# Unit 1's bonus sum in front of its masks, and unit 0's decayed k behind unit 2's bonus product

## The chip, the cores and the metric

One Trainium2 chip, one core. The metric is the device time of one execution in microseconds (us), median of several runs; lower is better. The kernel had been tuned already. Engines: TensorE (PE in the profile), VectorE (DVE), ScalarE (ACT), GpSimd (POOL), and SyncE (SP), which issues most transfers.

## The reference, cut to what matters

```python
def _attn_ref(r, k, v, w, u):            # B, H, S, D = 4, 8, 768, 48
    state = zeros(B, H, D, D)
    for t in range(S):
        cur = einsum('bhd,bhe->bhde', u * k_t, v_t)            # the "bonus" of the step itself
        y[:, :, t] = einsum('bhd,bhde->bhe', r_t, state + cur)
        state = w * state + einsum('bhd,bhe->bhde', k_t, v_t)
    return y

def _moe_ref(x, w_in, w_out):            # x: 3072 x 384, d_ff = 2048
    h = x @ w_in
    return (h * sigmoid(h)) @ w_out
```

The output is the second function applied to the first one's y. The kernel works on units, a unit being 128 steps of one batch (24 units, 4 for each stretch of 128 steps). For each it transposes r and k and scales them by powers of w, multiplies them to scores, masks the scores, multiplies by v to y, adds the bonus, transposes y and feeds it to the two dense layers. The bonus of a row is v times the sum over d of r·u·k.

## The kernel before

The parts that matter here; what each engine runs is in the order of emission.

```python
    def nat_ku(i):      # GpSimd
        nc.gpsimd.tensor_tensor(out=L["ku"], in0=kin[i % NIN][:, :, 0:D], in1=u_bc, op=ALU.mult)
    def nat_rk(i):      # GpSimd: the bonus product
        nc.gpsimd.tensor_tensor(out=L["rku_f"], in0=rin[i % NIN][:, :, 0:D], in1=L["ku"], op=ALU.mult)
    def nat_kc(i):      # GpSimd: decayed k, read by sums(i) only
        nc.gpsimd.tensor_tensor(out=kc[i % NKC][:, :, 0:D], in0=kin[n][:, :, 0:D], in1=lamC, op=ALU.mult)
    def bonus_sum(i):   # VectorE
        nc.vector.tensor_reduce(out=L["rku"], in_=L["rku_f"], axis=mybir.AxisListType.X, op=ALU.add)
    def bonus_vu(i):    # GpSimd
        nc.gpsimd.tensor_tensor(out=L["vu"], in0=vin[i % NIN], in1=L["rku"]...broadcast, op=ALU.mult)
    # p1(i): TensorE transposes r and k (tr, tk), VectorE scales both into rk
    # p2(i): TensorE scores ae, ao; VectorE masks them into am (two instructions)
    # p3y(i): TensorE y = am times v; p3e(i): VectorE y16 = y + vu
    # p4(i): TensorE transposes y16, ScalarE copies it to xT
    # fill(n): n portions of first- or second-layer matmuls; spin(n): n dummy matmuls
    # [...]
    bonus_act(0)
    nc.scalar.copy(out=st[1], in_=zero)
    win_part(512, 1024)
    p2(1, spins=2)
    bonus_sum(1)
    bonus_vu(1)
    p3e(0)
    nat_kc(0)
    spin(3)
    p3y(1)
    p3e(1)
    spin(2)
    p4(0)
    p1(2)
    nat_ku(2)
    nat_rk(2)
    win_part(1024, 1536)
    win_part(1536, 2048)
    nc.gpsimd.memset(rin[B][:, 0, 0:1], 0.0)   # holds the next loads back
    load(B)
    load(B + 1)
    p4(1)
    # [...]
    spin(2)
    fillers.extend(l1s(0, 0, 2))
    fill(.5)
    nat_v(2)
    bonus_sum(2)
    bonus_vu(2)
    p2(2)
    fill(1.5)
    p3y(2)
    # [...] later
    wout_part(0)
    sums(1)
    state(1)
    bonus_sum(b_)
    bonus_vu(b_)
    nat_kc(b_)
    wout_part(1)
```

Of the kernel before, what the change touches and what calls it, by code (L numbers as in the profile page):

```python
# [15 lines left out]
def kernel(  # L16
# [101 lines left out]
    def spin(n, t=None):  # L118

        if t is None:  # L120
            t = ps.tile([128, 512], FP, name="spin", tag="t", bufs=5)
        else:
            t = t.rearrange("s p t -> s (p t)")
        for _ in range(n):
            nc.tensor.matmul(t, junk[:, 0:128], junk, start=True, stop=True)
# [51 lines left out]
    def nat_ku(i):  # L177
        L = live.setdefault(i, {})
        L["ku"] = wrk.tile([128, H, D], FP, name="ku")
        nc.gpsimd.tensor_tensor(out=L["ku"], in0=kin[i % NIN][:, :, 0:D], in1=u_bc,  # L180
                                op=ALU.mult)

    def nat_rk(i):
        L = live[i]
        L["rku_f"] = wrk.tile([128, H, D], FP, name="rku_f")
        nc.gpsimd.tensor_tensor(out=L["rku_f"], in0=rin[i % NIN][:, :, 0:D], in1=L["ku"],  # L186
                                op=ALU.mult)

    def nat_kc(i):
        n = i % NIN  # L190
        nc.gpsimd.tensor_tensor(out=kc[i % NKC][:, :, 0:D], in0=kin[n][:, :, 0:D],  # L191
                                in1=lamC, op=ALU.mult)

    def bonus_sum(i):
        L = live[i]
        L["rku"] = wrk.tile([128, H], FP, name="rku", bufs=3)
        nc.vector.tensor_reduce(out=L["rku"], in_=L["rku_f"], axis=mybir.AxisListType.X,  # L197
                                op=ALU.add)

    def bonus_vu(i):  # L200
        L = live[i]
        L["vu"] = wrk.tile([128, H, D], FP, name="vu", bufs=3)
        nc.gpsimd.tensor_tensor(out=L["vu"], in0=vin[i % NIN],  # L203
                                in1=L["rku"].unsqueeze(2).broadcast_to([128, H, D]),
                                op=ALU.mult)
# [26 lines left out]
    def p1t(i):  # L232

        n = i % NIN
        L = live.setdefault(i, {})
        xs = [ps.tile([128, 2, NP, 64], FP, name="xs", tag="t", bufs=5) for _ in range(2)]
        for a, src in enumerate((rin, kin)):
            flat = src[n].rearrange("p h d -> p (h d)")
            for p in range(NP):
                for g in range(2):  # L240
                    t = slice(64 * g, 64 * g + 64)
                    nc.tensor.transpose(xs[g][0:PR, a, p, :],  # L242
                                        flat[t, 128 * p:128 * p + PR], ident[t, t])
        rk = wrk.tile([PR, 2, NP, C], FP, name="rk")
        L["rT"] = rk[:, 0]
        L["kT"] = rk[:, 1]
        L["xs"] = xs, rk

    def p1d(i):
        L = live[i]  # L250
        xs, rk = L["xs"]
        for g in range(2):
            nc.vector.tensor_tensor(out=rk[:, :, :, 64 * g:64 * g + 64], in0=xs[g][0:PR],  # L253
                                    in1=lam(g), op=ALU.mult)
# [6 lines left out]
    def p2(i, spins=0, nxt=None, late=False):  # L261
        L = live[i]
        ae = ps.tile([128, NP, C], FP, name="ae", tag="t", bufs=5)
        ao = ps.tile([128, NP, C], FP, name="ao", tag="t", bufs=5)
        spin(spins, ae)
        for p in range(NP):
            nc.tensor.matmul(ae[:, p, :], L["kT"][0:D, p, :], L["rT"][0:D, p, :],  # L267
                             start=True, stop=True)
            nc.tensor.matmul(ao[:, p, :], L["kT"][64:PR, p, :], L["rT"][64:PR, p, :],  # L269
                             start=True, stop=True)  # L270
        if nxt is not None:
            p1t(nxt)
        L["am"] = []
        for a in (ae, ao):
            am = wrk.tile([128, NP, C], F16, name="am", bufs=4)
            nc.vector.tensor_tensor(out=am, in0=a,  # L276
                                    in1=maskM.unsqueeze(1).broadcast_to([128, NP, C]),
                                    op=ALU.mult)
            L["am"].append(am)
        if nxt is not None and not late:  # L280
            p1d(nxt)

    def p3y(i):
        sc, b = unit(i)
        L = live[i]
        v16 = L["v16"]
        L["y"] = y = ps.tile([128, H, D], FP, name="y", tag="t", bufs=5)
        for p in range(NP):
            if sc:
                nc.tensor.matmul(y[:, 2 * p:2 * p + 2, :], L["rT16"][:, p, :],  # L290
                                 st16[b][:, p, :], start=True, stop=False)
            for j in range(2):
                nc.tensor.matmul(y[:, 2 * p + j, :], L["am"][j][:, p, :],  # L293
                                 v16[:, 2 * p + j, :], start=not sc,
                                 stop=(not sc or j == 1))

    def p3e(i):
        L = live[i]
        L["y16"] = wrk.tile([128, H, D], F16, name="y16")
        nc.vector.tensor_tensor(out=L["y16"], in0=L["y"], in1=L["vu"], op=ALU.add)  # L300
# [33 lines left out]
    def p4(i):  # L334
        sc, b = unit(i)
        L = live[i]
        if sc not in xts:
            xts[sc] = wrk.tile([128, NQ, B, C], F16, name="xT", bufs=3)
        yT = ps.tile([128, NQ, C], F16, name="yT", tag="t", bufs=5)
        yf = L["y16"].rearrange("p h d -> p (h d)")  # L340
        for q in range(NQ):
            nc.tensor.transpose(yT[:, q, :], yf[:, 128 * q:128 * q + 128], ident16)  # L342
        nc.scalar.copy(out=xts[sc][:, :, b, :], in_=yT)  # L343
# [68 lines left out]
    def win_part(c0, c1):  # L412
        nc.gpsimd.dma_start(out=win[:, :, c0:c1],
                            in_=moe_w_in[:, c0:c1].rearrange("(q p) n -> p q n", p=128))
# [27 lines left out]
    bonus_act(0)  # L442
    nc.scalar.copy(out=st[1], in_=zero)
    win_part(512, 1024)
    p2(1, spins=2)
    bonus_sum(1)
    bonus_vu(1)
    p3e(0)
    nat_kc(0)
    spin(3)  # L450
    p3y(1)
    p3e(1)
    spin(2)
    p4(0)
    p1(2)
    nat_ku(2)
    nat_rk(2)
    win_part(1024, 1536)
    win_part(1536, 2048)
    nc.gpsimd.memset(rin[B][:, 0, 0:1], 0.0)  # L460
# [174 lines left out]
```

## Time and profile before

| | before |
|---|---|
| median of the first 3 runs | 202.49 us (202.49 to 202.76) |
| TensorE busy | 193.5 of 201.0 us |
| unit 2's seven y matmuls start | 20.62 us |
| TensorE idle just before them | 0.40 us |

TensorE is nearly full, so the time is its work plus the few places where it waits. Of its 7.5 us without work, 4.5 lie in the first 66 us and the rest behind its last matmul. The prediction shows the lines.

### The profile page before, as it was taken

Reading aid. Unit: us, or ns where it says so; the run is one execution under the profiler, and the core shown is the slowest. Engines: PE = TensorE matmul, PEld = TensorE weight load, DVE = VectorE, ACT = ScalarE, POOL = GpSimd, SP = SyncE. Lnnn points to the kernel's source line nnn. Section 1 sums busy time; section 2 is a strip of 40 time slices with the busy share of each in tenths; the row PEclk is TensorE's granted clock in tenths of the full one; section 3 lists DMA queues with packets and bytes.
Section 4 is the critical chain, followed back from the end, with each engine's and each line's share of the span. In section 5 each row is a group of like instructions: output and inputs, shape, how many; then the busy total and the mean of one; then the engine's idle time right before and its main releaser. Section 6 shows DMA issues by size and latency. Waiting matters only on the chain.

```text
span 201.0 us, 5015 instructions
## 1 busy us (share of the span) xinstructions
PE 193.5 (96%) x1973; PEld 130.5 (65%) x1973; DVE 115.2 (57%) x233; ACT 98.0 (49%) x225; POOL 115.0 (57%) x145
## 2 busy tenths in 40 slices
PE   7989999999999999999999999999999999999993
PEld 2756778777766876675666765666764666744563
DVE  6686658885659439594646864646863635510121
ACT  2375587789232660139662038662029661069300
POOL 3479969979965764867683757481748370100000
PEclk9999999999999999999999999999999999999999
DMA  4999999999989961678731739201120001210022
GB/s 86 198 183 163 156 235 177 170 188 202 175 171 213 250 122 49 150 157 186 144 67 42 156 99 179 43 0 42 39 83 0 0 3 41 74 46 0 0 78 78
DMA packets 82207, 22.34 MB, mean 111 GB/s; under 512 B 75400, under 2 KB 82184, under 8 KB 82184
## 3 DMA queue, kind: packets, MB, share of 16 engines
q1 hardware_dynamic: 78504, 18.88, 43.9%
q0 software_dynamic: 3680, 3.15, 10.2%
q8 instruction: 15, 0.25, 0.5%
q14 instruction: 8, 0.07, 0.1%
HBM read 20.45 MB, written 4.72 MB: 125 GB/s over the span
## 4 chain that ended last, share of the span: by engine, by line
PE 84%; POOL 7%; issue 4%; DVE 2%; ACT 1%; POOLq 0%; DVEq 0%
PE ops L366 30%; PE hps L354 28%; PE ae L267 11%; PE xs L242 4%; PE y L293 2%; PE yT L342 2%; PE y L290 2%; POOL rku_f L186 2%; POOL ku L180 1%; PE sps L309 1%; PE ops L380 1%; DVE am L276 1%; POOL kc L191 1%; DVE y L300 1%; POOL vu L203 1%
## 5 line engine op out<-in xcount | busy, mean ns | idle before, releaser
L357 ACT ACTIVATE gT<-hps 128x256 f16<-128x256 f32 (+1 forms) x128 | 59.5, 493 | 24.6 <-PE hps L354 22.8
L354 PE MATMUL hps<-xT,win 128*128 128x256 f16 (+1 forms) x384 | 69.9, 326 | 0.9 <-ACT xT L343 0.4
L366 PE MATMUL ops<-wout,gT 128*128 128x384 f16 x368 | 65.5, 326 | 0.0
L354 PEld LDWEIGHTS <-win 128*128 128x128 f16 x384 | 35.1, 98 | 22.7 <-issue 1.7
L366 PEld LDWEIGHTS <-gT 128*128 128x128 f16 x368 | 34.3, 98 | 21.1
L343 ACT COPY xT<-yT 128x384 f16<-128x384 f16 x24 | 11.4, 476 | 58.2 <-PE yT L342 58.2
L276 DVE TENSOR_TENSOR am<-ae,maskM 128x512 f16<-128x512 f32 x24 | 16.6, 691 | 35.9 <-PE ao L269 35.8
L203 POOL TENSOR_TENSOR vu<-vin,rku 128x384 f32<-128x384 f32 x23 | 19.0, 828 | 19.9 <-DVE rku L197 19.8
L370 DVE COPY osb<-ops 128x384 f32<-128x384 f32 x23 | 12.8, 555 | 29.2 <-PE ops L366 29.0
L267 PE MATMUL ae<-rk 48*128 48x128 f32 x192 | 27.7, 285 | 0.0
L269 PE MATMUL ao<-rk 48*128 48x128 f32 x192 | 27.7, 285 | 0.0
L267 PEld LDWEIGHTS ae<-rk 48*128 48x128 f32 x192 | 23.1, 187 | 7.1 <-issue 5.5
L253 DVE TENSOR_TENSOR rk<-xs,pif 112x512 f32<-112x512 f32 x40 | 25.6, 680 | 1.7 <-PE xs L242 1.7
L186 POOL TENSOR_TENSOR rku_f<-rin,ku 128x384 f32<-128x384 f32 x24 | 24.1, 1005 | 1.9
L180 POOL TENSOR_TENSOR ku<-kin,u_bc 128x384 f32<-128x384 f32 x24 | 24.1, 1002 | 1.8 <-DMA kin<-in_k_dram 1.5
L191 POOL TENSOR_TENSOR kc<-kin,lamC 128x384 f16<-128x384 f32 x24 | 24.0, 1000 | 0.0
L269 PEld LDWEIGHTS ao<-rk 48*128 48x128 f32 x192 | 23.1, 187 | 0.0
L323 POOL CAST stb<-st 112x384 f16<-112x384 f32 x12 | 6.0, 502 | 25.9 <-DVE st L318 25.9
L300 DVE TENSOR_TENSOR y<-y,vu 128x384 f16<-128x384 f32 x24 | 13.3, 554 | 9.2 <-PE y L293 6.7
L276 DVE TENSOR_TENSOR am<-ao,maskM 128x512 f16<-128x512 f32 x24 | 16.3, 680 | 0.0
L197 DVE TENSOR_REDUCE rku<-rku_f 128x8 f32<-128x384 f32 x24 | 13.2, 550 | 2.8 <-POOL rku_f L186 2.4
L325 POOL TENSOR_TENSOR sdec<-st,pif 112x384 f32<-112x384 f32 x16 | 13.3, 835 | 2.2 <-ACT gT L357 1.1
(74 smaller groups left out, 190.5 us busy)
## 6 DMA issues: line engine op xcount, KB each, us to landing
rin<-in_r_dram SPq DMA_DIRECT2D x24, 192.0 KB, 3.7
kin<-in_k_dram SPq DMA_DIRECT2D x24, 192.0 KB, 3.9
vin<-in_v_dram SPq DMA_DIRECT2D x24, 192.0 KB, 3.7
out_dram<-osb SPq DMA_DIRECT2D x23, 192.0 KB, 2.0
win<-in_moe_w_in_dram POOLq DMA_DIRECT2D x4, 384.0 KB, 5.8
wout<-in_moe_w_out_dram POOLq DMA_DIRECT2D x2, 768.0 KB, 10.3
out_dram<-osh SPq DMA_DIRECT2D x1, 128.0 KB, 1.7
out_dram<-osh SPq DMA_DIRECT2D x1, 64.0 KB, 1.5
```

The lines of the kernel that those rows point to most:

```text
L180: nc.gpsimd.tensor_tensor(out=L["ku"], in0=kin[i % NIN][:, :, 0:D], in1=u_bc, op=ALU.mult)
L186: nc.gpsimd.tensor_tensor(out=L["rku_f"], in0=rin[i % NIN][:, :, 0:D], in1=L["ku"], op=ALU.mult)
L191: nc.gpsimd.tensor_tensor(out=kc[i % NKC][:, :, 0:D], in0=kin[n][:, :, 0:D], in1=lamC, op=ALU.mult)
L203: nc.gpsimd.tensor_tensor(out=L["vu"], in0=vin[i % NIN], in1=L["rku"].unsqueeze(2).broadcast_to([128, H, D]), op=ALU.mult)
L253: nc.vector.tensor_tensor(out=rk[:, :, :, 64 * g:64 * g + 64], in0=xs[g][0:PR], in1=lam(g), op=ALU.mult)
L267: nc.tensor.matmul(ae[:, p, :], L["kT"][0:D, p, :], L["rT"][0:D, p, :], start=True, stop=True)
L269: nc.tensor.matmul(ao[:, p, :], L["kT"][64:PR, p, :], L["rT"][64:PR, p, :], start=True, stop=True)
L276: nc.vector.tensor_tensor(out=am, in0=a, in1=maskM.unsqueeze(1).broadcast_to([128, NP, C]), op=ALU.mult)
L300: nc.vector.tensor_tensor(out=L["y16"], in0=L["y"], in1=L["vu"], op=ALU.add)
L354: nc.tensor.matmul(hps, win[:, q, ft * 128:(ft + 1) * 128], xts[sc][:, q, b0:b1, :].rearrange("p b t -> p (b t)"), start=(q == 0), stop=(q ...
L357: nc.scalar.activation(out=gts[sc][:, ft, b0 * C:b1 * C], in_=hps, func=AF.Silu)
L366: nc.tensor.matmul(ops, gts[sc][:, ft, b * C:(b + 1) * C], wout[:, ft, :], start=(ft == 0), stop=(ft == NFT - 1))
```

## The change

Its intent: GpSimd waits 1.2 us for unit 1's bonus sum, which stands behind two masks on VectorE; the sum is put in front of them. Unit 0's decayed k, which nobody needs soon, stands in front of unit 2's bonus product; it is put behind. One dummy matmul moves from behind unit 1's y to before it.

```diff
     bonus_act(0)
     nc.scalar.copy(out=st[1], in_=zero)
     win_part(512, 1024)
-    p2(1, spins=2)
     bonus_sum(1)
     bonus_vu(1)
+    p2(1, spins=2)
     p3e(0)
-    nat_kc(0)
-    spin(3)
+    spin(4)
     p3y(1)
     p3e(1)
-    spin(2)
+    spin(1)
     p4(0)
     p1(2)
     nat_ku(2)
     nat_rk(2)
+    nat_kc(0)
     win_part(1024, 1536)
```

## The prediction

> **What bounds the kernel now.** I read the page first, then the busy time by stages, the chain that ended last, and for 10 to 30 us the order of instructions on each engine. From the page:
>
> ```profile
> PE 193.5 (96%) x1973; PEld 130.5 (65%) x1973; DVE 115.2 (57%) x233; ACT 98.0 (49%) x225; POOL 115.0 (57%) x145
> PEclk9999999999999999999999999999999999999999
> ```
>
> TensorE is busy for 193.5 of 201.0 us at full clock. The busy time by stages tells where the missing 7.5 us lie:
>
> ```profile
> 0.00:20.00 20.00, 17.62 (x135) 10.99 (x135) 13.93 (x41) 10.10 (x28) 12.73 (x27) 1.00 0.88 158
> 20.00:60.00 40.00, 38.32 (x490) 30.57 (x490) 27.18 (x54) 26.43 (x73) 35.14 (x41) 1.00 1.06 184
> 100.00:150.00 50.00, 50.00 (x532) 32.74 (x531) 31.64 (x62) 20.25 (x41) 29.12 (x35) 1.00 0.32 76
> ```
>
> The first two times are the stretch and TensorE's busy part of it. TensorE lacks 2.4 us in the first 20, 1.7 us in the next 40 and nothing in the middle. The change touches only orders between 12 and 20 us, so the question is by how much TensorE's dense work after that starts earlier, and whether later waits swallow it. The chain that ended last, in order of time, says what the start hangs on:
>
> ```profile
> 12.99 0.74 POOL win L413
> 13.73 1.17 issue
> ...
> 14.95 0.82 POOL vu L203
> 15.77 0.97 POOL kc L191
> 16.73 0.96 POOL ku L180
> ...
> 17.78 1.01 POOL rku_f L186
> ...
> 18.81 0.04 DVE rku L197
> ...
> 19.28 1.29 DVE am L276 x2
> 20.57 0.05 issue
> 20.62 0.35 PE y L293 x7
> ```
>
> Until 20.6 us it runs through GpSimd, then over unit 2's bonus sum and two masks on VectorE to unit 2's y, and from there almost wholly through TensorE. VectorE's order of instructions has the two places that matter:
>
> ```profile
> 13.11 0.69 DVE L276 TENSOR_TENSOR am<-ae,maskM 128x512 f16<-128x512 f32 x1 [0.79 <-PE ao L269]
> 13.72 0.68 DVE L276 TENSOR_TENSOR am<-ao,maskM 128x512 f16<-128x512 f32 x1
> 14.31 0.54 DVE L197 TENSOR_REDUCE rku<-rku_f 128x8 f32<-128x384 f32 x1
> ...
> 18.81 0.55 DVE L197 TENSOR_REDUCE rku<-rku_f 128x8 f32<-128x384 f32 x1 [1.26 <-POOL rku_f L186]
> 19.28 0.68 DVE L276 TENSOR_TENSOR am<-ae,maskM 128x512 f16<-128x512 f32 x1
> ```
>
> Unit 1's sum waits behind unit 1's masks although its input was ready at 12.99 (the product ran 11.99 to 12.99); GpSimd waits 1.2 us for it. Unit 2's sum waits for GpSimd until 18.81, and unit 2's masks wait behind it although TensorE's last score matmul started at 18.63 and took 0.27, so that they could start at about 18.93. TensorE then idles for 0.40 us before unit 2's y at 20.62.
>
> **What the Trainium skill says.** "GPSIMD Engine Reference", section 3.1, gives about 2.6 cycles an element for two inputs: at its 1.2 GHz, 384 elements take 832 ns. The trace has 828 for vu, but 1,000 to 1,005 for ku, the k-r product and kc, whose inputs are padded rows; I use the trace's. "VectorE: DVE Perf Modes", section "The perf-mode tier table", gives tensor_reduce only its slowest mode; the trace has 0.54 us for the sum, and the next instruction starts 0.46 us after it, which is what moving it costs or frees. "TensorE: Matmul & The Clock Gate", Part 1, lets the clock fall after an idle window of some 3.4 us; the gaps here are 0.2 to 0.8 us and the granted clock is full in every slice, so I give a few tenths of idle no further price. "DMA: Bandwidth & Descriptors", section "Queues, rings and completion order", says that the DMA engines take turns between queues packet by packet; see the third rival.
>
> **The change part by part.** Nothing is added or removed: the dummy matmuls stay five (3 and 2 become 4 and 1), and the number of buffers taken and their order are the same.
>
> Part 1, unit 1's sum ahead of its masks. The sum starts at 13.02, just after its input (unit 2's started within 0.02 us of its own: 18.81 after 17.78 + 1.01). VectorE is idle from 12.3 to 13.11, so of its 0.46 us pitch 0.09 falls into idle time and the masks move from 13.11 to 13.49: 0.38 later. Masks at 13.49 and 14.09 to 14.78 (pitch 0.60), unit 1's y on TensorE at 14.84 instead of 14.46, done at 15.19. Unit 0's addition follows the masks at 14.69 instead of 14.77, so its transpose starts 0.08 earlier, at 15.30. On GpSimd the vu of unit 1 is free of its wait once the win issue is out (12.93 to 13.73): it runs 13.77 to 14.6 instead of 14.95 to 15.77. Unit 1's addition now waits for y and not for vu: 15.24 instead of 15.80, 0.56 earlier. The transposes of unit 2 go 0.08 earlier (15.47, 15.91), and VectorE's scalings of them run at 16.12 and 16.72 instead of 16.28 and 16.87. So 0.38 us is spent in front of y and what follows is still 0.08 to 0.16 earlier.
>
> Part 2, kc of unit 0 behind unit 2's product. kc takes 0.97 us of GpSimd; its only reader is unit 0's sums at 29.99, so it has over 10 us of slack. Unit 2's ku would start at 14.56, but its k has to land first. The view of DMA issues around 7.4 us has it:
>
> ```profile
> kin<-in_k_dram SPq DMA_DIRECT2D x1, 192.0 KB, 7.5
> ```
>
> Issued at 7.39, landed at about 14.9. So ku runs 14.95 to 15.95 (before: 16.73), the product 16.03 to 17.03 (before: 17.78 to 18.79), then kc to 18.0, the two win issues to 19.55, and the memset that opens the loads of units 4 and 5 at 19.6 instead of 20.29.
>
> Together, at unit 2: its sum no longer waits and follows the scalings at 17.3 to 17.86, in time in which VectorE was idle. The first layer's matmuls before unit 2's scores depend on unit 1's output copy, 0.08 earlier, so the last score is done at about 18.85. The masks start there instead of at 19.28: 0.43 earlier. They end at 20.13, and y comes at 20.19 instead of 20.62. vu of unit 2, 19.6 to 20.4, is ready before y ends at 20.54.
>
> TensorE's path from y on: before the change it idled for 0.22 at 26.07 (ScalarE's cast of v), 0.22 and 0.40 at 39.62 and 40.53, 0.27 at 48.41, 0.39 at 65.58, and not at all from there to 197. I followed each back: the cast runs behind gT, which waits for TensorE's own hps; the next two are y to addition to transpose and transpose to copy; the one at 48.41 goes through GpSimd's sdec and vu, which began at VectorE's state copies after unit 5's y; the last is ScalarE behind the transpose of unit 9. All hang on TensorE's earlier work, so they move with it and swallow nothing. The sum: 20.62 - 20.19 = 0.43 us, 202.49 - 0.43 = 202.06. I say 202.05.
>
> The parts aren't additive. Either alone takes most of unit 2's wait away. Part 1 alone leaves the product ready at about 17.6, still ahead of the scores; part 2 alone has it at about 17.83, and costs no delay of unit 1's masks.
>
> **Rivals.**
> 1. The wait only moves to unit 1: the masks' 0.38 us delay goes straight through to unit 2, and the result is 202.5 to 202.9. For it: y of unit 1 was on VectorE's masks already. Against it: before, 0.54 us of sum stood between masks and unit 0's addition, and unit 1's addition waited for vu until 15.80; both fall away.
> 2. A new wait at y of unit 2. If k lands a microsecond later than I read, ku starts at 15.9, the product ends at 18.0, still ahead of 18.85. If the masks wait instead on the first-layer matmuls before the scores, most stays. 202.1 to 202.3.
> 3. The DMA. The win parts and loads of units 4 and 5 start 0.7 us earlier. In before, DMA had a hole at 19 to 20.5 us (share 0.11 and 0.48) because these issues came late; it may be filled, or the win parts may take turns with unit 3's last loads. GpSimd waited 1.47 us for k of unit 4, until 27.40, but TensorE's transposes of it came only at 28.08. An earlier landing frees GpSimd and not TensorE: 202.0 to 202.1.
> 4. The whole 1.75 us by which the k-r product of unit 2 comes earlier reaches the end: 200.7. Against it, the scores' end at 18.85 is a floor that no order of GpSimd moves.
>
> **Range and chances.** The three runs of before lie 0.27 us apart, so a gain of 0.43 is little more than that. 201.7 holds a gain a little better than mine through the DMA; 202.6 holds rival 1 in part. Two per cent is 4 us, and TensorE lacks only 7.5 us in the whole span, most of it not touched. Faster or slower by that is 1 in 100 each.
>
> **What would show each step.** Right: unit 1's sum at 13.0 and masks at 13.5; vu of unit 1 at 13.8; ku of unit 2 at about 14.9 with a wait for k; unit 2's masks released by TensorE's scores and not by the sum, near 18.85; its y near 20.2; about 0.4 us less TensorE idle in the first 20.6 us and the same waits later. Wrong: unit 2's y still at 20.6; a new idle time of TensorE before 60 us, as on a load or on kc in unit 0's sums; or a span that differs by more than the shift of y.

## The result, and the profile after

| | before | changed |
|---|---|---|
| median | 202.62 us (202.49 to 202.83, 4 runs) | 202.14 us (202.14 to 202.26, 3 runs) |
| ratio, 95% | | 0.9977 (0.9958 to 0.9997) |
| profiled span | 201.0 us | 200.4 us |
| unit 2's y | 20.62 us | 20.02 us |

A ratio is the mean time of one kernel's runs over that of the other's of the same rounds, so not quite the ratio of the medians. One more run of the changed kernel took 223.65 us at a granted clock of 0.854 and is left out here; with it the median of the four is 202.2. The gain is 0.2%, and near the predicted 0.43 us (the medians differ by 0.48).

VectorE's order after, from the view of instructions in order of time (start, duration, what, and in brackets the idle time before it with what ended it):

```profile
12.85 0.55 DVE L197 TENSOR_REDUCE rku<-rku_f 128x8 f32<-128x384 f32 x1 [0.77 <-POOL rku_f L186]
13.32 0.68 DVE L276 TENSOR_TENSOR am<-ae,maskM 128x512 f16<-128x512 f32 x1
...
17.14 0.54 DVE L197 TENSOR_REDUCE rku<-rku_f 128x8 f32<-128x384 f32 x1
18.68 0.69 DVE L276 TENSOR_TENSOR am<-ae,maskM 128x512 f16<-128x512 f32 x1 [1.00 <-PE ao L269]
```

Unit 1's sum is now in front of the masks. Unit 2's sum (17.14) waits for nobody, and unit 2's masks are released by TensorE's scores and no longer stand behind the sum: VectorE was idle for 1.00 us before them. GpSimd, same view:

```profile
12.76 0.80 POOL L413 DMA_DIRECT2D win<-in_moe_w_in_dram  x1
13.58 0.84 POOL L203 TENSOR_TENSOR vu<-vin,rku 128x384 f32<-128x384 f32 x1
14.38 1.00 POOL L180 TENSOR_TENSOR ku<-kin,u_bc 128x384 f32<-128x384 f32 x1
15.46 1.01 POOL L186 TENSOR_TENSOR rku_f<-rin,ku 128x384 f32<-128x384 f32 x1
16.43 1.00 POOL L191 TENSOR_TENSOR kc<-kin,lamC 128x384 f16<-128x384 f32 x1
```

No bracket is left: the wait of 1.21 us before vu is gone, kc stands behind the product, and the product ends at 16.47 (before: 18.78). And TensorE at the two y:

```profile
14.06 0.20 PE L293 MATMUL y<-v,am 128*128 128x48 f16 x1 [0.25 <-DVE am L276]
14.66 0.35 PE L293 MATMUL y<-v,am 128*128 128x48 f16 x7 [0.40 <-DVE am L276]
...
20.02 0.35 PE L293 MATMUL y<-v,am 128*128 128x48 f16 x7 [0.27 <-DVE am L276]
```

Unit 1's y pays a new 0.25 us of idle time; unit 2's idles for 0.27 instead of 0.40.

**A part of the 0.60 us between the profiles is luck of the start.** Everything in the changed profile is 0.24 us early already at unit 0's first mask (9.14 against 9.38 us), long before the first changed instruction. The same four transposes of unit 0's r show why, before and then after:

```profile
5.37 1.06 PE L223 MATMUL tr<-ident,rin 128*112 128x128 f32 x4
```

```profile
5.10 0.60 PE L223 MATMUL tr<-ident,rin 128*112 128x128 f32 x4
```

Four equal instructions take 1.06 us in one run and 0.60 in the other. The Trainium skill, "TensorE: Matmul & The Clock Gate", Part 1, describes this: TensorE starts at half its clock until a free-running activity window has passed, so the moment differs from run to run. The traces show it: their record of the full clock begins 7.09 us after the start of the span before the change and 4.81 us after it. (The views print 1.00 for the time ahead of that record as well.) In 14 profiles the record begins between 4.35 and 7.59 us. Where it begins by 6.65 us, the first mask starts at 9.13 to 9.15 us; where it begins at 6.87 us or later, the mask starts at 9.26 to 9.44. So from here on my measure for this stage is **the time from unit 0's first mask to unit 2's seven y matmuls**: 20.62 - 9.38 = 11.24 us before, 20.02 - 9.14 = 10.88 after. The change is worth 0.36 us there; the other 0.24 of the profiles' 0.60 is the start. Behind that point nothing is lost or won: the waits of TensorE at 26.07, 39.62, 40.53, 48.41 and 65.58 us come back at 25.48, 39.03, 39.94, 47.82 and 65.00 with the same lengths to 0.01 us, and from unit 2's y to the end of the span it is 180.38 us in both.

One sign of the prediction did not show, "about 0.4 us less TensorE idle". Between the first mask and unit 2's seven y, TensorE's idle time by the record fell from 1.29 to 1.20 us only. Of the 0.36 us, 0.21 lie ahead of the first y matmul, and the record counts them as busy time: the first y started 1.18 us after the nine first-layer matmuls in front of it had begun (18.84 to 20.02), and starts 0.99 us after that now (18.58 to 19.57). The other 0.15 lie between the first y and the seven.

### The profile page after: what moved, and what is told of

Same layout as the page of the kernel before. It is cut to its first block, busy times and chain, and to the rows that moved or that the text cites. A ratio compares the mean times of both kernels' runs of the same rounds, so it can differ in the third digit from the quotient of the medians.

```text
span 200.4 us, 5014 instructions
## 1 busy us (share of the span) xinstructions
PE 192.2 (96%) x1973; PEld 129.8 (65%) x1973; DVE 115.1 (57%) x233; ACT 98.1 (49%) x225; POOL 115.1 (57%) x145
## 3 DMA queue, kind: packets, MB, share of 16 engines
q1 hardware_dynamic: 78504, 18.88, 43.7%
## 4 chain that ended last, share of the span: by engine, by line
PE 86%; issue 4%; POOL 4%; DVE 3%; ACT 2%; POOLq 0%; DVEq 0%
PE ops L366 30%; PE hps L354 29%; PE ae L267 11%; PE xs L242 4%; PE y L293 3%; PE yT L342 2%; PE y L290 2%; PE sps L309 1%; PE ops L380 1%; DVE am L276 1%; POOL rku_f L186 1%; POOL ku L180 1%; DVE y L300 1%; ACT xT L343 1%; PE ao L269 1%
```

## The experiments

Twelve kernels ran, all correct but the last, which is wrong on purpose (the record has no e9). A scatter of 0.3 to 2.5 us within one kernel remains in the timings (runs of the kernel before reach from 202.46 to 204.39 in these jobs), so the measure in the profile decides, and the times are given beside it. Each ratio is to the runs of before of the same job.

| kernel | measure (us) | median (us) | ratio to before, 95% |
|---|---|---|---|
| before | 11.24 | 202.67 (11 runs, first job) | |
| changed, run again (e12) | 10.83 | 202.23 | 0.9971 (0.9948 to 0.9993) |
| e1 sum (with the dummy) alone | 10.82 | 202.39 | 0.9976 (0.9952 to 1.0000) |
| e2 kc alone | 10.91 | 202.54 | 0.9989 (0.9969 to 1.0009) |
| e3 before, unit 2's sum behind its masks | 10.91 | 202.82 | 1.0011 (0.9987 to 1.0036) |
| e4 before, kc twice | 12.32 | 203.64 | 1.0035 (0.9997 to 1.0072) |
| e5 changed, two kc in front | 11.60 | 202.92 | 0.9998 (0.9967 to 1.0029) |
| e6 changed, three kc in front | 12.61 | 203.88 | 1.0047 (1.0009 to 1.0085) |
| e7 changed, dummies as before | 10.87 | 202.73 | 0.9999 (0.9977 to 1.0022) |
| e8 transposes of unit 2 first | 10.26 | 201.96 | 0.9958 (0.9922 to 0.9993) |
| e10 changed, weights issued early | 10.93 | 202.33 | 0.9969 (0.9945 to 0.9993) |
| e11 e8 with weights issued early | 10.26 | 202.00 | 0.9980 (0.9942 to 1.0019) |
| e13 e11 with loads left out | 10.21 | 201.61 | 0.9944 (0.9924 to 0.9964) |

In e8, e11 and e13 the seven matmuls follow the first of unit 2's y without a gap. Their start is taken as 0.20 us ahead of the next transposes, as it is after the change (20.02 and 20.22).

### e1: the first part alone

```diff
-    nat_kc(0)            # behind nat_rk(2), as in the changed kernel
+    nat_kc(0)            # in front of nat_ku(2), as in before
```

> Part 1 alone: unit 1's sum in front of its masks, unit 0's kc still in front of unit 2's product. My measure is the time from unit 0's first mask to unit 2's seven y matmuls: 11.24 us in before, 10.88 in the changed kernel. Theory (the scores' end is the floor, both parts overlap): the product ends about 1 us before the scores do, unit 2's masks are released by the scores, the measure is 10.88 within 0.1, and the time is 0.3 to 0.5 us under before. Rival (the move of kc is what pays): 11.2 and no gain.

The dummy matmul stays moved here as in the changed kernel, so this is the sum and the dummy together. Measured: 10.82, as in the changed kernel. Unit 2's sum waits 0.23 us for the product, until 17.65, and the masks start at 18.88, released by the scores. Sum and dummy take the whole stage gain; the rival falls. The median is 0.28 us under before.

### e2: the second part alone

```diff
 (kernel before)
     p3e(0)
-    nat_kc(0)
 ...
     nat_rk(2)
+    nat_kc(0)
```

> Part 2 alone: kc behind unit 2's product, unit 1's sum behind its masks as in before. Theory: vu of unit 1 stays late (its wait for the sum about 1.2 us stays), the product of unit 2 ends about 1.0 us earlier than in before, in front of the scores; the measure is 10.9 within 0.1 and the time 0.25 to 0.5 us under before. Rival (unit 1's sum is what pays): the measure stays at 11.2.

Measured: 10.91, so either part alone frees unit 2's masks. The median is only 0.13 us under before, not the 0.25 to 0.5 expected. In the profile a little is given back. vu of unit 2 stays late, unit 2's addition waits 1.01 us for it (until 20.99), and unit 3's y comes 16.46 us after the first mask, against 16.34 in the changed kernel and 16.28 in e1. The profile also met a wait that none before it had shown:

```profile
50.20 0.81 PE L366 MATMUL ops<-wout,gT 128*128 128x384 f16 x4 [0.28 <-DMA wout<-in_moe_w_out_dram]
```

TensorE waits for the second part of the second layer's weights. By the reckoning under e7 the ninth of these matmuls started 0.45 us late, and the profiled span is 201.0 us as before. This was not in my prediction; e7 and e10 to e13 go after it.

### e3: the wait itself taken away in another place

```diff
 (kernel before)
-    bonus_sum(2)
-    bonus_vu(2)
     p2(2)
+    bonus_sum(2)
+    bonus_vu(2)
```

> Before with one edit: unit 2's sum and vu behind its masks, nothing else moved. Theory: unit 2's masks were held by the sum alone, so they start with the scores, 0.35 us earlier, and y of unit 2 too (measure 10.9); but vu of unit 2 now waits for the late sum and ends near 21.5 us, so unit 2's addition, unit 3's scalings and scores come late and the gain is given back there: 0.0 to 0.2 us against before. Rival (the masks waited for the scores or something else): the measure stays at 11.2.

Measured: 10.91, and unit 3's y 16.86 after the first mask, 0.17 later than in before (16.69). The view of VectorE:

```profile
18.70 0.69 DVE L276 TENSOR_TENSOR am<-ae,maskM 128x512 f16<-128x512 f32 x1 [1.38 <-PE ao L269]
...
19.91 0.54 DVE L197 TENSOR_REDUCE rku<-rku_f 128x8 f32<-128x384 f32 x1
21.39 0.56 DVE L300 TENSOR_TENSOR y<-y,vu 128x384 f16<-128x384 f32 x1 [0.94 <-POOL vu L203]
```

With the sum out of their way the masks start with the scores: so in the kernel before it was the late sum, and through it GpSimd, that held them. The gain is then given back at unit 2's addition, as expected. Freeing the masks alone is worth nothing; vu has to come early too.

### e4, e5, e6: a known amount of GpSimd time in front of unit 2's product

```diff
 (e4: kernel before)          (e5, e6: changed kernel, kc in front of nat_ku(2), none behind)
     nat_kc(0)                +    nat_kc(0)      # e5: twice, e6: three times
+    nat_kc(0)                     nat_ku(2)
```

> Before with unit 0's kc computed twice (same result), in front of unit 2's product. Theory: GpSimd's chain into unit 2's sum was critical and what is lost there reaches the end one to one: measure 12.2 and time 203.5 to 203.7, about 0.97 us over before. Rival (later slack takes it up): under 0.4 us.

> The changed kernel with two kc of unit 0 in front of unit 2's product and none behind it. Theory: the product had about 2.2 us of slack to the scores' end less the sum's 0.46, so two kc (1.96 us) overshoot by 0.23 us: measure 11.1, time 0.1 to 0.3 us over the changed kernel. Rival (the slack is less, kc costs at once): 1 us or more.

> The changed kernel with three kc in front of unit 2's product. Theory: now GpSimd sets unit 2's masks again, 1.2 us later than in the changed kernel: measure 12.1, time 203.3 to 203.6. Rival (something else than sum or scores holds the masks): less than 0.6 us.

e4: two kc took 2.07 us instead of 0.99, 1.08 more, and the measure grew by 1.08. The profiles keep it to the end: unit 3's y comes 1.08 later too, and from the first mask to the end of the span it is 192.8 us for 191.6. So the chain through GpSimd was critical, one to one. By times this is weaker: the medians differ by 0.97, but the interval of the ratio just includes no change, as runs of before scatter up to 204.39.

e5 and e6 came out 0.5 above what I expected (11.60 and 12.61 for 11.1 and 12.1). Two causes show in the profiles. First, GpSimd itself started later in these two runs: its first work waits for unit 1's r to land, 8.00 and 7.90 us against 7.59 in the changed kernel's profile. Part 1 of the change has VectorE's masks of unit 1 wait behind a sum that waits for GpSimd, so this passes on (unit 1's sum at 13.25 in e5, 12.85 in the changed profile). Second, kc after kc took 1.08, not 0.98. The size was off, the mechanism was not:

```profile
18.93 0.55 DVE L197 TENSOR_REDUCE rku<-rku_f 128x8 f32<-128x384 f32 x1 [1.31 <-POOL rku_f L186]
19.40 0.68 DVE L276 TENSOR_TENSOR am<-ae,maskM 128x512 f16<-128x512 f32 x1
```

This is e5: the sum waits for GpSimd again and the masks follow it without a wait of their own, as in the kernel before. By dose, with 0, 1, 2 and 3 kc in front of the product the measure is 10.88, 10.82, 11.60 and 12.61: no cost for the first, 0.8 to 1.0 for each further one, the late starts included. The floor is TensorE's scores.

### e7: the dummy matmuls

```diff
-    spin(4)
+    spin(3)
     p3y(1)
     p3e(1)
-    spin(1)
+    spin(2)
```

> The changed kernel with the dummy matmuls as in before (3 and 2 and not 4 and 1). Theory: they lie in idle time of TensorE and do nothing: measure 10.88 within 0.1, time that of the changed kernel within 0.15 us. Rival (the fourth one keeps TensorE from something or warms it): a shift of one dummy matmul, 0.2 us.

The measure is 10.87, and yet the dummy matters. In this profile GpSimd was early by chance: unit 1's sum starts 3.55 us after the first mask and not 3.71 as in the changed kernel, its masks gain as much, but unit 2's scalings gain only 0.02 (6.78 for 6.80). TensorE shows where the rest was lost, first the changed kernel (its seven y start at 14.66), then e7:

```profile
14.85 0.38 PE L125 MATMUL spin<-junk 128*128 128x512 f16 x1
15.12 0.34 PE L342 MATMUL yT<-ident,y 128*128 128x128 f16 x3
```

```profile
14.48 0.35 PE L293 MATMUL y<-v,am 128*128 128x48 f16 x7 [0.40 <-DVE am L276]
14.67 0.59 PE L125 MATMUL spin<-junk 128*128 128x512 f16 x2
15.10 0.33 PE L342 MATMUL yT<-ident,y 128*128 128x128 f16 x3
```

Unit 0's output transposes (yT) start 0.46 us after unit 1's seven y with one dummy between them, 0.62 with two. From unit 1's sum to unit 2's y it is 7.17 us in the changed kernel, e1, e10 and e12, and 7.32 in e7. So behind the delayed y a second dummy costs 0.15 us, and moving it is a part of the gain. My expectation was wrong and the rival (0.2 us) about right; with the sum at 3.71, e7 would be at some 11.03 (an estimate, 3.71 + 7.32).

The median is 202.73, 0.34 over e1 in the same job. The profiled run, one of 202.44, also has the same wait as e2's:

```profile
48.29 1.46 PE L366 MATMUL ops<-wout,gT 128*128 128x384 f16 x8
49.92 0.81 PE L366 MATMUL ops<-wout,gT 128*128 128x384 f16 x4 [0.17 <-DMA wout<-in_moe_w_out_dram]
```

The ninth second-layer matmul needs the second half of the weights. Undisturbed, twelve of these take 2.11 us and the last 0.326, so one follows another after (2.11 - 0.326) / 11 = 0.162 us and the ninth starts 1.30 after the first: at 49.59 here. The weights landed at 49.84 (issued 38.04, 11.8 us). The same sum for the others: before, needed 50.21, landed 49.85; changed, needed 49.63, landed 49.57; e2, needed 49.75, landed 50.11. In these profiles the kernel before was 0.36 us clear of this wait and the changed one 0.06; e12, the changed kernel again, was 0.64 clear (needed 49.68, landed 49.04), so the clearance scatters from run to run. I had not looked for it, because a wait of zero length stands in no list.

Whether the dummy's 0.15 us and this wait make up all of e7's slower times is not shown: only one of its six runs was profiled.

### e12: the changed kernel again; e10: the weights issued earlier

```diff
 (e10)
     wout_part(0)
+    wout_part(1)
     sums(1)
     state(1)
     bonus_sum(b_)
     bonus_vu(b_)
     nat_kc(b_)
-    wout_part(1)
```

> The changed kernel again, unchanged, for more rounds beside e10 and e11 on one chip. Theory: the time to unit 2's y is the same in every run (measure 10.88 within 0.1), and what scatters is the start of TensorE and a wait for the second part of the second layer's weights near 49.7 us, which its profile missed by 0.05 us and e7, whose order is the same but for the dummies, hit by 0.2. So 202.1 to 202.9, median 202.3 to 202.5, and a profile that shows 0 to 0.3 us of idle there. Rival (the dummy split of e7 costs something): no run over 202.4.

> The changed kernel with the second part of the second layer's weights issued right behind the first, 2.5 us earlier on GpSimd. Theory (their landing is the next thing that TensorE runs into): landed at least 1 us before TensorE needs them, no wait there, measure 10.88 unchanged, median 0.05 to 0.3 us under that of e12. Rival (the wait is a chance of single runs, or the DMA engines are full and it lands no earlier): no difference from e12, or unit 5's vu comes late and costs 0.2.

e12 repeats the result: measure 10.83, median 202.23, five of six runs at 202.13 to 202.28 and one at 202.84. Its weights landed at 49.04, and TensorE had no wait there. The rival, a cost of e7's dummies, is right by e7's trace (0.15 us), and the medians point the same way (202.23 against 202.73, from different jobs); only its "no run over 202.4" failed.

e10 refutes my theory, as far as one profile can. The second part was issued 2.5 us earlier (35.6 for 38.14) and landed later, not earlier (50.1 for 49.04 in e12 and 49.57 in the changed kernel's first profile):

```profile
L417 POOL DMA_DIRECT2D wout<-in_moe_w_out_dram x2: 881/909/937, 34.6 to 35.6; - x2
...
DMA to landing us min/median/max: 10.1/12.3/14.5
```

This is e10's view of the weights' tile: the two issues start at 34.6 and 35.6, and the longest landing is the second's. 35.6 + 14.5 = 50.1 us, with 0.31 us of wait on TensorE. Nothing is gained by the issue: it only waits longer.

### e8: an attempt at a better version; e11: the same with the weights early

```diff
 (e8, on top of the change)
     p3e(1)
-    spin(1)
+    p1(2)
     p4(0)
-    p1(2)
 ...
-    fill(.5)
     nat_v(2)
     bonus_sum(2)
     bonus_vu(2)
     p2(2)
-    fill(1.5)
+    fill(2)
```

> An attempt at a better version on top of the change: unit 2's transposes on TensorE ahead of unit 0's output transposes, and the first layer's three matmuls before unit 2's scores put behind them. Theory (what bounds now is transposes, scalings, scores of unit 2): scalings about 0.45 us earlier, scores released by the scalings at about 16.9 us, measure 10.25 within 0.15, time about 0.6 us under the changed kernel, near 201.6. Rival (unit 0's and 1's output copies or the loads of unit 2 hold TensorE instead): no gain, or a loss of some tenths.

> The version of e8 (transposes of unit 2 first) with the weights issued early as in e10. Theory: measure 10.27 as in e8, no wait for the weights, 0.5 to 0.7 us under e12, near 201.7. Rival (the two gains don't add since the weights' issue delays unit 5): no better than e8's 201.96.

e8's measure is 10.26, 0.62 below the changed kernel, and unit 3's y comes 15.72 us after the first mask instead of 16.34. In the changed kernel the scores began at 17.49, behind three first-layer matmuls that had waited for unit 1's output copy (until 17.02); unit 2's scalings ended at 17.22. e8 moved both out of the way and dropped the dummy. About 0.40 of the 0.62 is the earlier scalings (6.40 after the first mask for 6.80), about 0.22 the three matmuls; the moves were not run apart. In time it has the lowest median of the correct kernels: 201.96 us (201.71 to 202.79), 0.4% under before. Against the changed kernel (202.23 in e12) the medians differ by 0.27 us, less than the 0.6 expected, and they come from different jobs. In the profiles the 0.6 reaches the end: from the first mask to the end of the span it is 190.7 us, and 191.3 and 191.2 in the two of the changed kernel.

e11 has the same measure, but not the gain expected (a median of 202.00 and not 201.7), and its runs scatter from 201.76 to 204.3. The profile fell on the 204.3 run, and shows where such a time comes from:

```profile
23.75 1.48 PE L354 MATMUL hps<-xT,win 128*128 128x256 f16 x12 [0.46 <-DMA win<-in_moe_w_in_dram]
...
51.80 0.81 PE L366 MATMUL ops<-wout,gT 128*128 128x384 f16 x4 [1.96 <-DMA wout<-in_moe_w_out_dram]
```

Now also the first layer's weights come late, and the second layer's by 1.96 us (issued 35.9, landed 51.8). The run is slow by its transfers.

### e13: fewer bytes in the way

```diff
 (e11, in load(i); the result is wrong on purpose)
+            if t is vin and NIN <= i < NIN + 4:
+                continue
```

> Wrong on purpose: e11 without the loads of v of units 6 to 9 (0.79 MB that share the DMA engines with the second layer's weights; the old contents of the buffers are used). Theory (the weights land when the DMA engines, full from 20 to 50 us at some 170 to 200 GB/s, have got through all of it, and not by when they are issued): the second part lands 2 us or more earlier than in e10 (50.1) and e11 (51.8), before 48 us; TensorE has no wait for it; the median is at 201.4 to 201.8, under e11's 202.0, with less scatter. Rival (the queue of GpSimd's DMAs is slow by itself): landing at 50 or later, a wait as in e11.

The median is 201.61 (201.5 to 202.31), and the profile lists no wait for weights. But the weights landed at about 49.2 us, not before 48: the expected 2 us against e10 did not come. And by the sum under e7 they were needed at 48.95, so the 0.3 us by which the twelve matmuls take longer (2.41 for 2.11) are likely a wait that the list does not show. The trial does not separate the theories. SyncE's queue moved up by what was left out, and the DMA engines stayed at least as full until 45 us (the two last figures of these stretches are their mean busy share, which this view can print above 1, and GB/s):

```profile
40.00:45.00 5.00, 5.00 (x69) 4.27 (x68) 4.18 (x10) 4.97 (x15) 4.65 (x6) 1.00 1.27 184
```

In e11 the same five microseconds have 1.27 and 184; over 20 to 50 us it is 1.11 and 188 here, 1.09 and 182 there. That the landing is set by what the DMA engines have to move is therefore plausible and not shown.

## Why the prediction was right

**The size and the mechanism.** Predicted 202.05 and a gain of 0.43. Measured by medians 202.14 and 0.48, by the stage 0.36 (0.41 in e12), by the ratio 0.23%. Unit 2's masks were held by its sum and are now held by its scores: the brackets show it, e3 shows it without touching GpSimd, and e4 shows that the chain before it passed on one to one. That the medians come so near to 0.43 is partly luck: the profiled run of 202.14 had the early start worth 0.24 us.

**Part 1.** Counted from the first mask, the sum was predicted at 3.64 us and came at 3.71, the masks at 4.11 and 4.18, unit 1's y at 5.46 and 5.52, unit 2's scalings at 6.74 and 6.80, unit 2's masks at 9.47 and 9.54, its y at 10.81 and 10.88. The whole row is 0.07 late, from its first member on: GpSimd's product of unit 1 ended 0.07 later, counted from the first mask, than in the profile of before (12.82 - 9.14 against 12.99 - 9.38). The rest of the working held to 0.02. It holds with the dummy moved: the prediction gave the new split no price, and e7 shows that the old one costs 0.15 us. And the prediction read a granted clock "full in every slice" off the page; by the trace's record the full clock began at 7.09 us.

**Part 2.** One step failed, without effect: ku of unit 2 was to wait until 14.95 for its k. It ran at 14.38 with no wait, since k had landed at 14.3 in that run (issued 7.50, 6.8 us). With over 1 us of slack behind it, this changed nothing. In e11 it did wait, 0.45 us until 14.83.

**Not additive.** As predicted, either part alone takes the masks' wait away (e1 and e2: 10.82 and 10.91). What I didn't predict is that they are unequal later: only part 1 brings vu of unit 2 forward enough, and part 2 alone loses 0.12 us at unit 3's y. In these runs e1 (the sum and the dummy) does all that the change does.

**The rivals.** The first (the delay of unit 1's masks goes through) is seen in small: unit 1's y idles for 0.25 us more, and with the dummy moved nothing of it reaches unit 2. The fourth (all of the product's 1.75 us) fell against the floor of the scores. But this floor is not one "that no order of GpSimd moves": unit 2's scores now follow unit 1's sum at a fixed distance, and with it GpSimd. In e5, where the sum came 0.40 later than in the changed kernel, the scores came 0.39 later. The third, the DMA, I sized too low. "They move with it and swallow nothing" was true of the waits that I had followed, and it overlooked one that had no length yet: the second layer's weights, 0.36 us clear in before. In the two profiles of the change itself it took nothing; in e2, e7, e10 and e11 it took 0.2 to 2 us.

**Open.** What sets the landing of those weights. By e10's one profile it is not the time of issue. Full DMA engines would fit the profiles, and e13 failed to separate that from a slow queue. The Trainium skill, "DMA: Bandwidth & Descriptors", section "Issuing engines are not separate DMA queues", has all issuers share the same 16 engines; the landing 10.8 to 15.9 us after issue agrees with sharing, but no run here varied it alone.

## What to carry to other kernels

When an engine's in-order queue holds an instruction that waits, look at what stands behind it and could run: here two masks stood behind a sum, and what ended the sum's wait lay on a third engine. Work out the floor that takes over (the scores, 0.4 us further on) before pricing a removed wait; 1.75 us of earlier product was worth 0.36. When two runs agree in a sum, compare its terms: e7's equal measure hid a loss of 0.15 us behind an earlier GpSimd. And when the busy engine is about to come earlier everywhere, check every transfer for how long before its use it lands, as one that is just in time stands in no list of waits.

## What the Trainium skill lacked or had wrong

- "TensorE: Matmul & The Clock Gate", Part 1: it has the warm-up that differs from run to run, and the traces agree. But it puts the spread at 500 ns to either side; in the 14 profiles here the record of the full clock begins 3.1 to 6.3 us after TensorE's first matmul (4.35 to 7.59 us, the first matmul being at 1.26 us in all). The cost to unit 0's first mask was up to 0.3 us (9.13 to 9.44).
- "GPSIMD Engine Reference", section 3.1: the estimate of 832 ns worked out from it fits vu (820 to 840 ns, its second input a broadcast), not ku, the product and kc (990 to 1,020 ns, two full inputs, one of them in padded rows). No run separated the padding from the broadcast, and the page prices neither.
- "DMA: Bandwidth & Descriptors", section "Anatomy of one DMA": its fit of 2.0 us plus bytes at 436 GB/s gives an estimate of 3.8 us for the 786,432 bytes of a part of the second layer's weights. Beside the other loads it took 8.9 to 15.9 us here, and in e10 an issue 2.5 us earlier landed no earlier. The section has no figure for DMA engines that are already full.
